# Second stage of a long convolution: one of the four spectral products goes to PSUM instead of SBUF

## Chip, cores and metric

The kernel runs on one core of one Trainium2 chip. The metric is the device time of one execution in microseconds, as the median of several executions.

## The reference, cut to what matters

```python
h_filt = (np.maximum(pos_emb @ w1, 0.0) @ w2) * np.exp(-0.01 * np.arange(S))[:, None]
u = x * v                                    # (2, 12480, 128)
Uf = np.fft.rfft(u, n=2 * S, axis=1)
Hf = np.fft.rfft(h_filt, n=2 * S, axis=0)
y = np.fft.irfft(Uf * Hf[None], n=2 * S, axis=1)[:, :S]
t = (x * y).reshape(B * S, D)                # 24960 tokens of 128
h = t @ w_in                                 # 128 -> 2048
out = (np.maximum(h, 0) + alpha * np.minimum(h, 0)) @ w_out
```

A long convolution per channel, done as a product of spectra, is followed by a two-layer network over all tokens. The change sits in the complex product `Uf * Hf`.

## The kernel before, in words

**Stages.** The transform has length 128 x 179 and is split by its two coprime factors, so that no twiddle step is needed between them. Stage 1 transforms over 179 and keeps frequencies `f` from 0 to 89 (`NF = 90`). Stage 2, for each `f`, transforms over 128, multiplies the spectra of data and filter, and stores the product again as two fp16 halves in the SBUF tile `z`. Stages 3 and 4 go back. The network of 32 token blocks and 16 slices of the hidden layer (lines 1247 to 1361) follows and takes most of the time. The 128 channels are worked on in two groups of 64, so there are two rounds of stage 2.

**Stage 2.** The function `stage2` (line 847) steps through the frequencies two at a time (`f0`). `skew` (line 151) writes out a software pipeline in program order. In each iteration it issues, in this order, `low`, `high`, `total`, `transform`, `neg`, `more` and `load`, each for a different `f0`: `low` for the pair that `transform` had three iterations before, `high` two before, `total` one before. One iteration holds:

- `transform`: 24 matmuls of 192 columns (lines 878 to 883) into a PSUM tile `p` of two banks. Bank 0 holds the real plane and bank 1 the imaginary plane, each with 256 columns of data (2 batches x 64 channels x 2 frequencies) and 128 of the filter. There are three such tiles, `mm`.
- `hidden` (line 894): ScalarE copies the filter part, scaled and repeated for both batches, to an SBUF tile `hs`.
- `product` (line 906): VectorE multiplies both planes of `p` by the real plane of `hs` into `ta`, then both planes by the imaginary plane of `hs` into `tb`. Each is one operation over 512 elements in each partition. `ta` and `tb` lie in SBUF (the tile named `ring` in the rows).
- `total`: `real` (line 911, GpSimd) subtracts `tb[1]` from `ta[0]`, and `imaginary` (line 916, VectorE) adds `tb[0]` to `ta[1]`; 256 elements each.
- `high` (line 929, ScalarE) and `low` (line 933, GpSimd) split the sum into two fp16 halves.
- `neg` (line 845, ScalarE) negates the table of sines for the transform two iterations on.
- `more`: one step of other work. In the first round it is `weights_in`, which rebuilds the network's first weights from their 64-bit words in `later(read, 6)` (four groups of six iterations; lines 592 to 598) and scales them in `later(halves, 3)` (four groups of three; lines 602 to 607). In the second round it is `unscale` (lines 1138 to 1153).

The first and last pairs need care. The last two pairs of a round are worked on in pieces by `end`, in an order that a small planner (`Plan`) fixed beforehand.

**PSUM.** Three tiles `mm` take two banks each, and `mb[0]` and `mb[1]` take one each. In stage 2 the first round writes columns 0 to 15 of `mb[0]` by matmul (line 598) and uses columns up to 47 on VectorE (line 618 and the helper `scales`). The second round writes columns 0 and 1 by matmul (line 1148) and copies them on VectorE (line 1153). `mb[1]` holds the words under repair.

**Order.** Every engine works through its own list in program order. No wait is written in the code: the framework places a wait where an instruction uses a tile that another engine has written or still reads.

Of the kernel before, what the change touches and what calls it, by code (L numbers as in the profile page):

```python
# [14 lines left out]
ALU = mybir.AluOpType  # L15
# [21 lines left out]
NU = B * CG  # L37
# [252 lines left out]
def body(ctx, tc, A, out, stop=None, dbg=None):  # L290
    nc = tc.nc
    sy, ac, ve, po, te = nc.sync, nc.scalar, nc.vector, nc.gpsimd, nc.tensor
# [34 lines left out]
    def units(u, n=1, p=128):  # L327
        assert u >= FIRST or u + n <= FIRST
        t, u = (ring, u - FIRST) if u >= FIRST else (first, u)
        return t[:p, u:u + n].rearrange("p u e -> p (u e)")  # L330
# [348 lines left out]
    def phase_a():  # L679
        ps = ctx_a.enter_context(tc.tile_pool(name="psa", bufs=1, space=PSUM))  # L680
        mm = [ps.tile([128, 1024], F32, name=f"mm{j}") for j in range(3)]
        mb = [ps.tile([128, 512], F32, name=f"mb{j}") for j in range(2)]
# [164 lines left out]
        def stage2(tu, au, bu, hu, nu, extra, loaded=0):  # L847

            st = {}
            tws = {}  # L850

            def load(f0):
                if f0 % FB == 0:
                    fb = f0 // FB
                    tws[fb] = table(tu, fb)
                    if fb >= loaded:
                        load_table(tu, fb)
# [6 lines left out]
            def transform(f0):  # L864
                ns = st.pop(("ns", f0))
                tw = tws[f0 // FB]
                x = f0 // 2
                p = mm[((NF - 2) // 2 - x) % 3].rearrange("p (a m) -> p a m", a=2)
                for j in range(2):
                    f1 = f0 + j  # L870
                    fi = f1 % FB
                    ch, cl, sh, sl = (tw[:, fi, m, :] for m in range(4))
                    nh, nl = ns[:, j, 0, :], ns[:, j, 1, :]
                    zc = [z[:, :, m, 0, f1, :] for m in range(2)]
                    zs = [z[:, :, m, 1, f1, :] for m in range(2)]
                    for pl, (ah, al, bh, bl) in enumerate(((ch, cl, nh, nl), (sh, sl, ch, cl))):
                        o = p[:, pl, :2 * NC].rearrange("p (b f c) -> p b f c", f=2, c=ZC)[:, :, j]
                        te.matmul(o, ah, zc[0], start=True, stop=False)
                        te.matmul(o, ah, zc[1], start=False, stop=False)
                        te.matmul(o, al, zc[0], start=False, stop=False)  # L880
                        te.matmul(o, bh, zs[0], start=False, stop=False)
                        te.matmul(o, bh, zs[1], start=False, stop=False)
                        te.matmul(o, bl, zs[0], start=False, stop=True)
                st["p", f0] = p, *(units(u[x % n]).rearrange("p (a m) -> p a m", a=2) for u, n in ((hu, 2), (au, 4), (bu, 2)))
                if f0 < NF - 4:
                    hidden(f0)
                    product(f0)

            def hidden(f0, b0=0, b1=NB):

                p, hs, _, _ = st["p", f0]
                h = p[:, :, 2 * NU:2 * NC]
                if b1 - b0 == NB:
                    ac.activation(hs.rearrange("p a (b m) -> p a b m", b=B), h.unsqueeze(2).to_broadcast([128, 2, B, 2 * CG]), AF.Copy, scale=2.0 ** -17)  # L894
                    return
                for b in range(B):
                    x, y = (min(max(k - b * NB // B, 0), NB // B) for k in (b0, b1))
                    if x < y:
                        at = b * 2 * CG
                        ac.activation(hs[:, :, at + x * 2 * ZC:at + y * 2 * ZC], h[:, :, x * 2 * ZC:y * 2 * ZC], AF.Copy, scale=2.0 ** -17)  # L900

            def product(f0, b0=0, b1=NB):
                p, hs, ta, tb = st["p", f0]
                m = slice(b0 * 2 * ZC, b1 * 2 * ZC)
                for t, a in ((ta, 0), (tb, 1)):
                    ve.tensor_tensor(out=t[:, :, m], in0=p[:, :, m], in1=hs[:, a:a + 1, m].to_broadcast([128, 2, (b1 - b0) * 2 * ZC]), op=ALU.mult)  # L906

            def real(f0, b0=0, b1=NB, e=po):
                _, _, ta, tb = st["p", f0]
                m = slice(b0 * 2 * ZC, b1 * 2 * ZC)  # L910
                e.tensor_tensor(out=ta[:, 0, m], in0=ta[:, 0, m], in1=tb[:, 1, m], op=ALU.subtract)  # L911

            def imaginary(f0, b0=0, b1=NB):
                _, _, ta, tb = st["p", f0]
                m = slice(b0 * 2 * ZC, b1 * 2 * ZC)
                ve.tensor_tensor(out=ta[:, 1, m], in0=ta[:, 1, m], in1=tb[:, 0, m], op=ALU.add)  # L916

            def total(f0):
                real(f0)
                imaginary(f0)  # L920

            def place(f0, b0, b1):

# [14 lines left out]
            def until(last, stage):  # L938
                return lambda f0: stage(f0) if f0 <= last else None

            skew(list(range(0, NF, 2)), (9, until(NF - 10, low)), (8, until(NF - 8, high)), (7, until(NF - 6, total)),
                 (6, until(NF - 4, transform)), (4, neg), (4, more), (0, load))

            def end(P):
# [3 lines left out]
                P.now, P.pace["end"] = ("end", 0), (-1e5, 0)  # L948
                room = {f0: P.buf("mm") for f0 in (NF - 2, NF - 4)}
                P.op("PE", 1990, lambda: transform(NF - 2), w=[room[NF - 2], "zh"])  # L950
                lows = []

# [3 lines left out]
                def some(what, f0, x=None):  # L956
                    b0, b1 = ((0, 1), (1, NB), (0, NB))[2 if x is None else x]
                    n, a, y = 4 * ZC * (b1 - b0), (f0, b0, b1), ("y", f0, x)
                    e, en = (ve, "DVE") if x == 0 or x and f0 == NF - 2 and what == "low" else (po, "POOL")
                    ns = dve_ns if e is ve else pool_ns  # L960
                    if what == "product":
                        op("ACT", act_ns(n, True) + 100 * (x == 1), lambda: hidden(*a), [room[f0]], [("hs", f0, x)])
                        op("DVE", 2 * dve_ns(n), lambda: product(*a), [room[f0], ("hs", f0, x)], [y, ("product", f0, x)])
                    elif what == "total":
                        op(en, ns(n / 2), lambda: real(*a, e), [y], [(y, 0)])
                        op("DVE", dve_ns(n / 2), lambda: imaginary(*a), [y], [(y, 1)])
                    elif what == "high":
                        op("ACT", act_ns(n), lambda: high(*a), [(y, 0), (y, 1)], [y])
                    else:
                        op(en, ns(n), lambda: low(*a, e), [y], [("low", f0, x)])  # L970
                        lows.append(("low", f0, x))
# [97 lines left out]
        with tc.tile_pool(name="pre", bufs=2) as pre:  # L1069
# [15 lines left out]
            if stop == 'p':  # L1085
                return
        end = stage2((7, 0, 3, 5), (18, 16, 17, 19), (20, 21), (22, 23), 14, weights_in(mb, 9, (11, 12, 13, 24), (2, 10), 2))
        for g in range(1, NG):
            P = Plan(mm=3, m=2, x=7, v=3, sq1=2, uhl=3, sn=2, gst=2)
            P.flow = 360 / 255  # L1090
            y = end(P)
            P.guard = {"sq1": [("product", f0, x) for f0 in (NF - 4, NF - 2) for x in range(2)]}
            later = stage1(P, g, True, dict(x=(13, 5, 6, 7, 8, 3, 4), v=(2, 0, 1), uhl=(10, 11, 12), sq1=(22, 23)))
            drain(paced(P, "h", islice(later, 3)))
            drain(paced(P, "s", stage3(P, g - 1, [lambda u=u: units(u, 4) for u in (14, 18)], lambda i: units((24, 9)[i]), y)), paced(P, "u", later))
            tables = (0, 3, 14, 16)
            P.op("DMA", 2 * dma_ns(128 * 4096), lambda: [load_table(tables, fb) for fb in range(2)], w=["tw"])
            P.after("x")
            P.after("v")
            negs = 22  # L1100
            raws = [ring[:, u - FIRST:v - FIRST + 1:v - u] for u, v in ((6, 7),)]
            for f0 in range(0, 2 * FB, 2):
                P.op("ACT", 520, lambda f0=f0: negate(tables, negs, f0), r=["tw"])
                P.after("sq1")
            P.pace.update(h=(-30228, 41505), s=(-14272, 7297), u=(23122, 6183))
            P.urge, P.patience, P.bias = 3.1, 0, 911
            P.run()
            rotate(P)
            if stop == 'r':
                return  # L1110
            end = stage2(tables, (8, 20, 21, 5), (9, 18), (10, 11), negs, chain([none] * 4, [lambda: load_words(raws, 0)], unscale(mb)), 2)
# [336 lines left out]
```

## Time and profile before

| what | value |
|---|---|
| median of 3 runs | 1636.32 us (1633.52 to 1636.78) |
| the profiled execution | 1634.51 us |
| its span, first to last instruction | 1632.7 us |
| mean granted TensorE clock | 0.982 of full speed |
| busy: TensorE, ScalarE, VectorE, GpSimd | 95%, 81%, 79%, 63% of the span |
| first round of stage 2 | about 143 to 243 us of the span |
| second round of stage 2 | about 374 to 461 us of the span |

The rows of the trace name an instruction by engine, line and tile. In the timeline's rows the first number is the start in microseconds from the span's start and the second the time taken, over all instructions of the row where `x2` or more stands at its end. A bracket gives how long the engine was idle before and what ended that. Instructions of one engine overlap a little, so the distance from start to start says more of the cost of a link in a chain than the duration does.

### The profile page before, as it was taken

What the parts mean: (1) busy time and instruction counts of PE and PEld (TensorE: products, weight loads), DVE (VectorE), ACT (ScalarE), POOL (GpSimd) and SP (SyncE); (2) the same over time, 40 slices, a digit from 0 to 9 for tenths busy, and PEclk for the clock granted to TensorE, in tenths of its full rate; (3) what the DMA queues carried; (4) which work ended last, traced back from release to release, by engine and by line L of the source; (5) the groups of instructions that cost most, each with busy time, mean ns of one, the idle gap of its engine ahead of it and who ended that gap; (6) DMA issues with size and microseconds to landing.
All of it is one profiled execution on the core that took longest, in us unless ns stands there. A gap on an engine that the chain in (4) does not pass through costs nothing.

```text
span 1632.7 us, 34281 instructions
## 1 busy us (share of the span) xinstructions
PE 1553.0 (95%) x13452; PEld 1094.6 (67%) x13452; DVE 1289.7 (79%) x1867; ACT 1328.3 (81%) x2203; POOL 1033.0 (63%) x728
## 2 busy tenths in 40 slices
PE   6888887999998999999999999999999999999998
PEld 3888887889987566666666666665666666666664
DVE  7898988998998777777777777777777777777775
ACT  5887786886876888888888888888888888888886
POOL 5697896987972665556655556555566555665554
PEclk8998998999999999999999999999999999999999
DMA  7353437775358321202112021220202202022000
GB/s 203 113 173 133 143 119 217 238 215 172 130 153 234 100 56 41 57 21 57 47 50 57 21 57 36 61 57 21 57 21 76 57 20 57 21 76 57 20 11 20
DMA packets 91663, 141.86 MB, mean 87 GB/s; under 512 B 7057, under 2 KB 59891, under 8 KB 90061
## 3 DMA queue, kind: packets, MB, share of 16 engines
q1 hardware_dynamic: 90525, 139.10, 29.6%
q8 instruction: 105, 1.72, 0.4%
q10 hardware_dynamic: 976, 0.57, 0.1%
q14 instruction: 57, 0.47, 0.1%
HBM read 99.02 MB, written 40.63 MB: 86 GB/s over the span
## 4 chain that ended last, share of the span: by engine, by line
PE 72%; DVE 13%; POOL 4%; issue 4%; ACT 3%; DMA 3%; SPq 0%; POOLq 0%; DVEq 0%; ACTq 0%
PE hp L1270 31%; PE o L1270 31%; DVE ring L906 5%; DVE ring L916 2%; DMA first<-in_xv 2%; POOL ring L758 1%; PE yp L280 1%; PE yp L281 1%; PE yp L282 1%; PE mm L1007 1%; PE mm L1009 1%; PE mm L1008 1%; POOL ring L749 1%; DVE ring L1024 1%; POOL ring L721 1%
## 5 line engine op out<-in xcount | busy, mean ns | idle before, releaser
L1347 POOL TENSOR_TENSOR g_lo<-ring,g_hi 128x780 f16<-128x780 f32 x288 | 480.9, 1674 | 474.0 <-ACT g_hi L1346 474.0
L1340 DVE SCALAR_TENSOR_TENSOR ring<-ring,keep,hp 128x780 f32<-128x780 f32 x512 | 524.8, 1025 | 268.1 <-ACT ring L1339 258.8
L1339 ACT ACTIVATE ring<-hp 128x780 f32<-128x780 f32 x512 | 418.7, 818 | 162.3 <-PE hp L1270 161.0
L1270 PEld LDWEIGHTS <-w 128*128 128x128 f16 x3840 | 368.5, 97 | 269.3 <-issue 13.4
L1270 PE MATMUL hp<-ah,w 128*128 128x390 f16 x1984 | 489.2, 328 | 0.3 <-DVE ring L1340 0.3
L1346 ACT ACTIVATE g_hi<-ring 128x780 f16<-128x780 f32 x512 | 433.5, 847 | 1.1 <-DVE ring L1340 1.1
L1270 PE MATMUL o<-g_hi,ring 128*128 128x390 f16 x1536 | 378.4, 328 | 1.1 <-ACT ot L1361 1.0
L1270 PEld LDWEIGHTS <-ring 128*128 128x128 f16 x2304 | 223.2, 97 | 160.4 <-issue 2.1
L1270 PE MATMUL hp<-alo,w 128*128 128x390 f16 x992 | 244.7, 328 | 0.8 <-DVE alo L363 0.8
L1347 DVE TENSOR_TENSOR g_lo<-ring,g_hi 128x780 f16<-128x780 f32 x224 | 230.2, 1028 | 0.0
L1270 PE MATMUL o<-g_lo,ring 128*128 128x390 f16 x768 | 189.6, 328 | 0.6 <-POOL g_lo L1347 0.6
L1250 POOL TENSOR_TENSOR gl<-gt,gh 90x1024 f16<-90x1024 f32 x62 | 153.5, 2475 | 1.3 <-ACT gh L1249 1.3
L906 DVE TENSOR_TENSOR ring<-mm,ring 128x512 f32<-128x512 f32 (+2 forms) x188 | 116.0, 656 | 16.4 <-ACT ring L894 16.3
L1270 PE MATMUL o<-g_hi,w 128*128 128x390 f16 x512 | 126.3, 328 | 0.0
L1007 PE MATMUL mm<-t,z 128*128 128x128 f16 x512 | 102.7, 233 | 10.2 <-ACT z L929 6.8
L933 POOL TENSOR_TENSOR z<-ring,z 128x512 f16<-128x512 f32 x88 | 105.6, 1201 | 3.4 <-ACT z L929 3.4
L1009 PE MATMUL mm<-t,z 128*128 128x128 f16 x512 | 101.8, 231 | 0.7 <-DVE z L933 0.7
L1008 PE MATMUL mm<-t,z 128*128 128x128 f16 x512 | 101.9, 231 | 0.0
L911 POOL TENSOR_TENSOR ring<-ring 128x256 f32<-128x256 f32 (+1 forms) x90 | 77.1, 857 | 31.2 <-DVE ring L906 30.9
L804 ACT ACTIVATE z<-mm 128x720 f16<-128x720 f32 (+1 forms) x99 | 73.6, 753 | 23.1 <-PE mm L794 22.0
L807 DVE TENSOR_TENSOR z<-mm,z 128x720 f16<-128x720 f32 (+1 forms) x99 | 85.2, 875 | 6.1 <-ACT z L804 5.8
L792 PE MATMUL mm<-t,ring 98*128 98x180 f16 x320 | 80.1, 254 | 10.1 <-DVE ring L520 3.1
(214 smaller groups left out, 3141.7 us busy)
## 6 DMA issues: line engine op xcount, KB each, us to landing
gt<-g_d SPq DMA_DIRECT2D x16, 1440.0 KB
g_d<-ring SPq DMA_DIRECT2D x28, 720.0 KB
ring<-in_tw SPq DMA_DIRECT2D x34, 512.0 KB
ring<-in_xv SPq DMA_DIRECT2D x72, 196.0 KB
xt<-in_xt SPq DMA_DIRECT2D x31, 390.0 KB
out_t<-ot SPq DMA_DIRECT2D x31, 390.0 KB
first<-in_xv SPq DMA_DIRECT2D x56, 196.0 KB
first<-in_tw SPq DMA_DIRECT2D x12, 512.0 KB
```

The costliest lines, as they stand in the source:

```text
L807: ve.tensor_tensor(out=zb[:, 1, :, x:y, cs], in0=pv()[:, :, x:y], in1=zb[:, 0, :, x:y, cs], op=ALU.subtract)
L906: ve.tensor_tensor(out=t[:, :, m], in0=p[:, :, m], in1=hs[:, a:a + 1, m].to_broadcast([128, 2, (b1 - b0) * 2 * ZC]), op=ALU.mult)
L933: e.tensor_tensor(out=zl, in0=v, in1=zh, op=ALU.subtract)
L1007: te.matmul(o, hi, t3[:, 0], start=True, stop=False)
L1008: te.matmul(o, hi, t3[:, 1], start=False, stop=False)
L1009: te.matmul(o, lo, t3[:, 0], start=False, stop=True)
L1250: po.tensor_tensor(out=dl, in0=src, in1=dh, op=ALU.subtract)
L1270: te.matmul(o[:, b, :TOK], w, d[:, b], start=start and n == 0, stop=stop and n == 2)
L1339: ac.activation(neg, h, AF.Relu, scale=-1.0)
L1340: ve.scalar_tensor_tensor(out=acts[n], in0=neg, scalar=keep[:, f:f + 1], in1=h, op0=ALU.mult, op1=ALU.add)
L1346: ac.activation(gh, a, AF.Copy)
L1347: (po if n % 2 or n % NFT == 0 else ve).tensor_tensor(out=gl, in0=a, in1=gh, op=ALU.subtract)
```

## The change

In the iterations before the last two pairs, `products` takes the place of `product`. The product `p[0] * hs[1]`, which only the imaginary sum reads, goes to columns 256 to 511 of the PSUM tile `mb[0]`, by an operation of its own. The other product with `hs[1]` becomes an operation of 256 elements too. The imaginary sum in `total` then adds `ta[1]` from SBUF and `cross` from PSUM.

```diff
             st = {}
             tws = {}
+            cross = mb[0][:, 2 * NU:4 * NU]
...
                 if f0 < NF - 4:
                     hidden(f0)
-                    product(f0)
+                    products(f0)
...
+            def products(f0):
+                p, hs, ta, tb = st["p", f0]
+                m = slice(0, 2 * NU)
+                ve.tensor_tensor(out=cross, in0=p[:, 0, m], in1=hs[:, 1, m], op=ALU.mult)
+                ve.tensor_tensor(out=ta, in0=p[:, :, m], in1=hs[:, :1, m].to_broadcast([128, 2, 2 * NU]), op=ALU.mult)
+                ve.tensor_tensor(out=tb[:, 1], in0=p[:, 1, m], in1=hs[:, 1, m], op=ALU.mult)
...
             def total(f0):
+                ta = st["p", f0][2]
                 real(f0)
-                imaginary(f0)
+                ve.tensor_tensor(out=ta[:, 1], in0=ta[:, 1], in1=cross, op=ALU.add)
```

`2 * NU` is 256. `product` and `imaginary` stay as they are for the last two pairs of a round. There are 43 pairs before them in each round, 86 in all.

## Rows read from the trace of the kernel before

**Rows 1.** The page, part 4: chain that ended last, by engine.

```profile
PE 72%; DVE 13%; POOL 4%; issue 4%; ACT 3%; DMA 3%; SPq 0%; POOLq 0%; DVEq 0%; ACTq 0%
```

**Rows 2.** Windows: stretch, its length, busy us (instructions) of each engine, PEclk, DMA share, GB/s.

```profile
143.00:205.00 62.00, 55.22 (x667) 53.39 (x666) 56.20 (x100) 47.45 (x89) 51.47 (x51) 1.00 0.40 137
205.00:243.00 38.00, 33.68 (x395) 32.38 (x393) 32.83 (x54) 32.58 (x69) 36.70 (x37) 1.00 0.36 118
386.00:461.00 75.00, 75.00 (x912) 75.00 (x910) 73.72 (x116) 61.23 (x114) 74.91 (x76) 1.00 0.36 116
```

**Rows 3.** Timeline of VectorE in round one, a group of six iterations.

```profile
174.30 1.29 DVE L906 TENSOR_TENSOR ring<-mm,ring 128x512 f32<-128x512 f32 x2 [1.75 <-ACT ring L894]
175.50 0.69 DVE L558 TENSOR_SCALAR mb<-mb 128x512 f32<-128x512 f32 x1
176.10 0.57 DVE L916 TENSOR_TENSOR ring<-ring 128x256 f32<-128x256 f32 x1
176.59 1.28 DVE L906 TENSOR_TENSOR ring<-mm,ring 128x512 f32<-128x512 f32 x2
...
182.37 0.67 DVE L567 SCALAR_TENSOR_TENSOR ring<-ring,mb 128x512 int32<-128x512 int32 x1
...
188.79 1.29 DVE L906 TENSOR_TENSOR ring<-mm,ring 128x512 f32<-128x512 f32 x2 [1.61 <-ACT ring L894]
```

**Rows 4.** Timeline of ScalarE, end of the same group.

```profile
187.01 0.65 ACT L592 ACTIVATE mb<-ring 128x512 f32<-128x512 f32 x1 [1.75 <-DMA ring<-in_wi]
```

**Rows 5.** Groups of VectorE by line and shape: busy us, mean ns, idle before.

```profile
L906 DVE TENSOR_TENSOR ring<-mm,ring 128x384 f32<-128x384 f32 x8 | 4.0, 546 | 0.0
...
L561 DVE TENSOR_SCALAR mb<-mb 128x512 int32<-128x512 int32 x4 | 2.7, 684 | 0.0
...
L906 DVE TENSOR_TENSOR ring<-mm,ring 128x128 f32<-128x128 f32 x8 | 1.9, 281 | 0.0
```

**Rows 6.** Timeline of VectorE in round two.

```profile
388.38 1.28 DVE L906 TENSOR_TENSOR ring<-mm,ring 128x512 f32<-128x512 f32 x2
...
460.07 1.27 DVE L906 TENSOR_TENSOR ring<-mm,ring 128x512 f32<-128x512 f32 x2
```

**Rows 7.** Timeline of TensorE in round two: the first of every six matmuls.

```profile
388.04 0.25 PE L878 MATMUL mm<-z,ring 128*128 128x192 f16 x1
...
440.02 0.25 PE L878 MATMUL mm<-z,first 128*128 128x192 f16 x1
```

**Rows 8.** Timelines of VectorE and TensorE early in the kernel.

```profile
23.30 0.30 DVE L455 TENSOR_SCALAR nb<-ones,n 128x128 f32<-128x128 bf16 x1
...
23.91 0.16 DVE L337 TENSOR_SCALAR sr<-mb 128x1 int32<-128x1 int32 x1
...
24.21 0.46 PE L468 MATMUL mb<-w2q,nb 128*128 128x128 f32 x2 [1.97 <-DVE sr L337]
```

**Rows 9.** Timelines of TensorE and ScalarE around the last group that reads words.

```profile
198.25 0.25 PE L598 MATMUL mb<-ones,first 128*128 128x1 bf16 x4 [1.11 <-ACT first L597]
...
204.99 0.58 ACT L894 ACTIVATE ring<-mm 128x512 f32<-128x512 f32 x1
```

**Rows 10.** Timelines of TensorE and VectorE at the start of round two.

```profile
384.53 0.60 PE L1148 MATMUL mb<-one,first 1*128 1x1 f32 x4 [0.91 <-DVE first L1144]
...
386.39 1.28 DVE L906 TENSOR_TENSOR ring<-mm,ring 128x512 f32<-128x512 f32 x2
```

**Rows 11.** Timeline of ScalarE: the filter's copy at the end of round one.

```profile
219.01 0.60 ACT L894 ACTIVATE ring<-mm 128x512 f32<-128x512 f32 x1 [0.17 <-PE mm L883]
...
233.62 0.58 ACT L894 ACTIVATE ring<-mm 128x512 f32<-128x512 f32 x1
...
241.07 0.58 ACT L894 ACTIVATE ring<-mm 128x512 f32<-128x512 f32 x1
```

**Rows 12.** Timeline of GpSimd at the end of round one.

```profile
238.47 1.34 POOL L933 TENSOR_TENSOR z<-ring,z 128x512 f16<-128x512 f32 x1
239.77 0.73 POOL L911 TENSOR_TENSOR ring<-ring 128x256 f32<-128x256 f32 x1
```

## The prediction, made before the change was run

> **What bounds the kernel now.** The chain that ended last comes first. TensorE holds 72% of it and VectorE 13% [rows 1]; nearly all of the TensorE share is the network, which this change does not touch. So only the two rounds of stage 2 can move, and the windows say how much is there. Round two is full: TensorE 75.0 us busy of 75, VectorE 73.7, GpSimd 74.9 [rows 2]. Round one has room: in its first 62 us TensorE is busy 55.2 and VectorE 56.2, in the next 38 us 33.7 and 32.8 [rows 2]. The timelines then tell which wait ends last.
>
> In round two the same matmul comes back from 388.04 to 440.02 after 105 sets of six, so 0.495 us a set and 1.980 us for the 24 matmuls of an iteration [rows 7]. VectorE's pair of products comes 36 times from 388.38 to 460.07, every 1.991 us [rows 6]. TensorE sets the pace; VectorE is slower by 0.011 us, 0.4 us behind at the end.
>
> The first 62 us of round one are groups of six iterations, 174.30 to 188.79, 14.49 us, where six transforms need 11.9 [rows 3, 7]. Four iterations carry a word operation of VectorE each, and the last, line 567, ends at 183.04 [rows 3]. Only then can the next words be loaded; ScalarE waits 1.75 us for them until 187.01 [rows 4], and what it has queued behind, the filter's copy for the next pair, starts the next group. So a group is 8.74 us of VectorE and 5.75 of load and ScalarE. After the words are read, groups of three iterations follow. Two of them take 219.01 to 233.62, 14.61 us [rows 11]; the copies of line 602 on ScalarE and the matmul of line 603, which waits for them, set these 7.3 us, and neither uses what the change moves.
>
> **VectorE's part of the change.** Two products of 512 start 1.20 us apart from the next instruction, so 0.60 each [rows 3]. The sizes 128 and 384 take 281 and 546 ns [rows 5], 1.035 ns an element, so 256 elements take 0.60 less 256 x 1.035 ns: 0.335 us from start to start. A new iteration has 0.335 + 0.60 + 0.335 = 1.27 for 1.20: **0.07 more**. Two prices are not in the trace. Writing the product to PSUM: 0.335 at the least, 0.60, a full product, at the most; I take 0.335, since line 561, which writes PSUM, takes 684 ns where line 906 steps and lasts about the same (1.29 for two overlapping) [rows 3, 5]. The sum from SBUF and PSUM: 0.335 at the least, as for a product of one operand from each, and 0.49 at the most, what the sum of line 916 steps now [rows 3]. Something holds up this sum of two SBUF operands while GpSimd works: in round two 1.991 - 1.20 = 0.79 us are left for it and its wait for an operand, far over 0.335 for its size, while the products, with one operand in PSUM, keep 1.27 to 1.29 a pair in both rounds [rows 3, 6]. I take 0.335. So the sum saves **0.155 us** in a word iteration and **0.45** in round two.
>
> **What this is worth where VectorE sets the pace.** From a group's start to the end of line 567 there are four products and three sums: 4 x 0.07 - 3 x 0.155 = -0.19 us. Three groups are followed by a load: **-0.6 us**.
>
> **A wait that the change adds.** Line 598's matmuls write columns of `mb[0]`, the bank that `cross` now shares. The trace shows how such a wait is placed [rows 8]: line 468 writes columns 0 to 127 of a tile `mb` from `nb`, ready at 23.60, yet it waits for line 337, which reads column 384 of that tile until 24.07, and starts at 24.21. So I take the order to be by bank: line 598, and line 1148 in round two, wait for the `cross` product that precedes them in program order, and 24 matmuls of the next transform stand behind them on TensorE.
>
> The Trainium skill bears on this ("PSUM — Partial Sum Buffer", section "PSUM bank collisions raise a hardware error"): two engines in one bank and 32-partition quadrant are to be kept apart by semaphores, whatever columns they use. By that rule the sum is the -0.2 us below; with waits by column it would be the first rival's -3.3.
>
> *Line 598, followed by a load (three times).* The sixth pair of a group now starts 10.43 us after the group's start (four iterations of 1.27 + 0.60 + 0.335 and one of 1.605); its `cross` ends about 0.4 later, at 10.85. TensorE then needs 0.15, one transform (1.98) and 0.25 to give ScalarE the next filter part at 13.2. ScalarE does not ask before it has the words and has split the pair before: in rows 3 and 4 that is about 0.65 us before the pair at 188.79 (the copy takes 0.58 [rows 9]), so near 188.1, 13.8 after the start, and 13.6 when the group is 0.19 shorter. So the load hides the wait with 0.4 us to spare: **0**.
>
> *The last group.* No load follows. Line 598 ran at 198.25 [rows 9]. With the group starting 0.6 earlier, at 188.2 for 188.79 [rows 3], `cross` ends at 199.0 and the matmul runs at 199.1, 0.8 late. The three transforms behind it end at 205.4, where ScalarE's copy began at 205.0 [rows 9]. So the next part begins **0.4 us late** (the 0.6 saved is in this figure).
>
> *Line 1148.* It ran at 384.53 behind line 1144; the pair of its iteration starts at 386.39 [rows 10] and `cross` ends near 386.8. TensorE stands 2.3 us longer, the next pair moves from 388.38 to about 390.2, **+1.8**.
>
> **The rest of round one.** The groups of three keep their pace. After 233.62 nothing of line 602 is left, and the next three copies of the filter, at best 1.98 us apart, take until 241.07 [rows 11]: 7.45 against 5.94. GpSimd is late there: lines 933 and 911 at 238.47 and 239.77 follow each other without a gap [rows 12]. Their 1.34 and 0.73 become about 1.16 and 0.60 without the sum of line 916, and the line 911 that ended at 240.50 ends near 239.2: **-1.3**. The last such sum ends the round **0.3** sooner.
>
> **The rest of round two.** 36 iterations at 1.980 instead of 1.991: **-0.4**. At the tail the last iteration is 1.27 + 0.335 long for 1.991: **-0.4**.
>
> **Sum:** round one +0.4 - 1.3 - 0.3 = -1.2; round two +1.8 - 0.4 - 0.4 = +1.0; together **-0.2 us**. Stage 3 and the second stage 1 start from these ends, so I pass it on in full. The profiled execution would take 1634.3 for 1634.51, and the median of the runs shown lies 1.8 above that: **1636.1 us**.
>
> **Rivals.**
>
> *Waits by column.* Then lines 598 and 1148 wait for nothing new. Round one: -0.6, the last group's four iterations -0.3, then -1.6 as above: -2.5. Round two -0.8. Sum -3.3: **1633.0**. Against it stands the wait of line 468 [rows 8].
>
> *The matmul wait is not hidden (slower).* It decides from the point where `cross` ends more than 0.4 us later than I put it, or where ScalarE is ready sooner. Then TensorE, not the load, sets the start of three groups. Line 598 comes 1.4 us later than now in its group (10.9 for 9.5 after the start); if that counts whole, three groups add 4.1 to the sum of -0.2: +3.9, **1640.2**. For it: six transforms fill 11.9 of 14.5 us and TensorE has no other slack. Against: 1.75 us of waiting for words [rows 4].
>
> *The prices at their upper end.* Product 0.60 and sum 0.49 make a word iteration 0.34 longer than now and round two 2.03 an iteration, over TensorE's 1.98: 16 x 0.34 + 36 x 0.05 + 1.0 = +8: **1644**. The two sizes measured speak against it [rows 5].
>
> *GpSimd gives back more.* Freed of line 916, the groups of three may also shorten, at most by what lies between 14.61 and two times 6.2 (three transforms and a matmul), 2.2 us a pair of groups; half of that twice gives -2.4: **1633.7**.
>
> **How the numbers follow.** Changes under 0.2% (3.3 us) can hardly be told from none here. Forecast 0.62; waits by column 0.10; wait not hidden 0.15; upper prices 0.03; GpSimd gives more 0.10. The likeliest is 1636.1, with 1634 to 1638.5 as its own range, two microseconds or so for the parts of its sum. The range that leaves out 2 in 10 reaches from the first rival, less 0.5 for the size of its parts, to the second: 1632.5 to 1640.2. The first rival lies on the bound of 3.3 us, so half of it counts as faster, and half of the last, whose parts may come out larger, with 0.02 from the forecast's edge: 0.12. The second and third rivals, less 0.02 for their near ends, are slower: 0.16. Same: 0.72.
>
> **What the profile will show.** Right: the sum of line 916's place near 0.42 us everywhere, the 256-element products near 0.41; line 911 near 0.6; line 598 and line 1148 waiting for VectorE's `mb` product; groups still near 14.4 us and ended by the load; round two's pairs 1.98 apart with VectorE idle for some 0.37 of them. Wrong: a `mb` product of 0.6 us; line 598 without a wait on VectorE; a group that starts when TensorE is done; a round two that starts no later.

## The result, and the profile after

The changed kernel takes 1644.15 us as the median of 7 runs (1641.72 to 1655.02); the kernel before, run beside it on the same chip, took 1633.8 (7 runs). The ratio is **1.0073, 95% interval 1.0054 to 1.0091**. The forecast was no change, with a range up to 1640.2 us, 0.24% over its base of 1636.32: the kernel is slower, and by more than the range allows.

The kernel before is called before here, the changed one after. The profiled execution of after took 1648.78 us, 4.6 over the median; its span is 1647.0 us. To see where the time came from, measure each round of stage 2 on ScalarE, from the start of its first filter copy (line 894 before, 895 after) to the start of its 43rd. What lies outside (the head before the first copy, the stretch between the rounds, the tail) differs by up to 6 us between profiles of kernels that are alike there, so only the two lengths are compared. In after the first round runs from 146.24 to 251.11 us, the second from 383.30 to 472.16:

| kernel | first round | second round | slow stretches | ratio to before, 95% interval |
|---|---|---|---|---|
| before | 98.53 | 85.61 | 0 + 0 | |
| after | 104.87 | 88.86 | 3 + 1 | 1.0073 [1.0054, 1.0091] |
| e1_own_bank | 99.03 | 84.75 | 0 + 0 | 1.0004 [0.9991, 1.0017] |
| e2_wait_only | 102.81 | 88.74 | 2 + 1 | 1.0046 [1.0029, 1.0063] |
| e3_filler | 100.59 | 87.26 | 0 + 0 | 1.0032 [1.0016, 1.0049] |
| e4_round2_free | 103.35 | 84.60 | 2 + 0 | 1.0034 [1.0018, 1.005] |
| e5_order | 101.93 | 90.39 | 2 + 1 | 1.0049 [1.0032, 1.0067] |
| e6_more_first | 107.18 | 88.90 | 3 + 1 | 1.0091 [1.0076, 1.0107] |
| e7_all | 105.87 | 84.60 | 2 + 0 | 1.0067 [1.0052, 1.0082] |
| e8_between | 95.37 | 86.93 | 0 + 1 | 0.9998 [0.9982, 1.0014] |
| e9_between_all | 92.95 | 83.93 | 0 + 0 | 0.9968 [0.9956, 0.9981] |
| e10_round2_only | 97.11 | 84.61 | 0 + 0 | 0.9997 [0.9986, 1.0009] |
| e11_between_before | 96.69 | 85.47 | 0 + 0 | 0.9992 [0.9983, 1.0001] |

The lengths are of one profile each. The column of slow stretches counts, for the first round + the second, how often TensorE ran at 1.2 GHz behind line 598 (of four times) and behind line 1157 (of one); both are explained below. Round one of one and the same program differs by about 1.5 us between profiles, for two reasons: its groups end with a load that takes longer or shorter (before 98.53, e10 97.11), and where line 598 waits, the clock falls behind some of the waits and not behind others (after 104.87 with three slow stretches, e4 103.35 with two).

After loses 6.34 us in the first round and 3.25 in the second. The windows over the same stretches as in [rows 2] show what became of the engines (columns: stretch, its length, then each engine's busy time and number of instructions, the granted TensorE clock, DMA share, GB/s):

```profile
143.00:205.00 62.00, 53.78 (x612) 52.71 (x611) 49.58 (x112) 44.27 (x81) 39.84 (x44) 0.94 0.35 123
...
386.00:461.00 75.00, 71.61 (x847) 71.22 (x845) 61.37 (x148) 57.12 (x105) 63.74 (x71) 0.98 0.36 127
```

VectorE and GpSimd are busy for less of both stretches than in [rows 2], and so is TensorE, whose clock averages 0.94 in the first 62 us. TensorE's waits between 140 and 480 us (who waits for whom: us in total, times, the longest) name the place:

```profile
PE mb L598 <- DVE mb L912: 10.1, 4, 2.6
...
PE mb L1157 <- DVE mb L912: 3.4, 1, 3.4
```

Both are the waits of [rows 9, 10]'s matmuls for the new `mb` product. Before the change, line 598 stood for ScalarE instead, and for 6.5 us less:

```profile
PE mb L598 <- ACT first L597: 3.6, 4, 1.1
```

TensorE's timeline of after shows what follows the new waits:

```profile
160.71 0.24 PE L598 MATMUL mb<-ones,first 128*128 128x1 bf16 x4 [2.62 <-DVE mb L912]
160.81 0.24 PE L879 MATMUL mm<-z,ring 128*128 128x192 f16 x1
160.89 0.24 PE L880 MATMUL mm<-z,ring 128*128 128x192 f16 x1
...
161.30 0.37 PE L884 MATMUL mm<-z,ring 128*128 128x192 f16 x1
161.46 0.37 PE L879 MATMUL mm<-z,ring 128*128 128x192 f16 x1
...
164.60 0.25 PE L881 MATMUL mm<-z,ring 128*128 128x192 f16 x1
164.69 0.25 PE L882 MATMUL mm<-z,ring 128*128 128x192 f16 x1
...
396.50 0.91 PE L1157 MATMUL mb<-one,first 1*128 1x1 f32 x4 [3.39 <-DVE mb L912]
...
397.63 0.37 PE L881 MATMUL mm<-z,ring 128*128 128x192 f16 x1
397.80 0.37 PE L882 MATMUL mm<-z,ring 128*128 128x192 f16 x1
```

The first matmuls behind the wait are 0.08 us apart, the next twenty 0.16, then 0.08 again. TensorE had stood 2.62 us, and the granted clock of 160.8 to 164.8 is 0.57 of full speed: most of this transform ran at 1.2 GHz instead of 2.4. ScalarE shows that this transform, and no longer the load, now starts the group:

```profile
161.62 0.63 ACT L592 ACTIVATE mb<-ring 128x512 f32<-128x512 f32 x1 [1.43 <-DMA ring<-in_wi]
...
164.65 0.60 ACT L895 ACTIVATE ring<-mm 128x512 f32<-128x512 f32 x1 [1.84 <-PE mm L884]
```

The words are there at 161.62; the filter copy waits for TensorE (line 884) until 164.65. The third group differs: behind its wait of 2.22 us the clock stays full (1.00 from 193 to 197 us), and the filter copy waits for TensorE for only 0.35 us. The three groups that a load follows last 16.38, 15.72 and 15.06 us, start to start of line 558, where before's lasted 14.47, 14.63 and 14.49; the one that no load follows 15.79 for 12.81.

VectorE (groups of instructions: busy us, mean ns of one, then the idle time before them; below it two starts of the timeline):

```profile
L913 DVE TENSOR_TENSOR ring<-mm,ring 128x512 f32<-128x512 f32 x86 | 58.5, 681 | 0.0
...
L912 DVE TENSOR_TENSOR mb<-mm,ring 128x256 f32<-128x256 f32 x86 | 37.2, 433 | 42.8 <-ACT ring L895 39.8
...
L914 DVE TENSOR_TENSOR ring<-mm,ring 128x256 f32<-128x256 f32 x86 | 35.7, 415 | 0.0
L929 DVE TENSOR_TENSOR ring<-ring,mb 128x256 f32<-128x256 f32 x86 | 35.4, 411 | 0.1
```

```profile
167.15 0.41 DVE L929 TENSOR_TENSOR ring<-ring,mb 128x256 f32<-128x256 f32 x1
167.66 0.43 DVE L912 TENSOR_TENSOR mb<-mm,ring 128x256 f32<-128x256 f32 x1
168.00 0.68 DVE L913 TENSOR_TENSOR ring<-mm,ring 128x512 f32<-128x512 f32 x1
```

The prices are as forecast: 433, 415 and 411 ns. But from the sum to the next `mb` product it is 0.51 us, where a 256-element operation otherwise lets the next one start after 0.34: VectorE waits for its own sum before it overwrites the columns that the sum reads. Word iterations are 2.38 us apart (2.29 before, 2.205 in the forecast).

### The profile page after: what moved, and what is told of

The parts are those of the page before. It is cut to its first block, busy times and chain, and to the rows that moved or that the text cites. A ratio compares the mean times of both kernels' runs of the same rounds, so it can differ in the third digit from the quotient of the medians.

```text
span 1647.0 us, 34371 instructions
## 1 busy us (share of the span) xinstructions
PE 1561.4 (95%) x13452; PEld 1102.7 (67%) x13452; DVE 1279.6 (78%) x1953; ACT 1330.0 (81%) x2203; POOL 1019.3 (62%) x728
## 4 chain that ended last, share of the span: by engine, by line
PE 76%; POOL 7%; DVE 7%; ACT 4%; DMA 3%; issue 2%; POOLq 0%; SPq 0%; ACTq 0%; DVEq 0%
PE hp L1279 31%; PE o L1279 30%; POOL z L942 3%; POOL ring L919 2%; PE mm L1016 1%; PE mm L1018 1%; PE yp L280 1%; PE yp L281 1%; PE yp L282 1%; PE mm L1017 1%; POOL ring L758 1%; DVE z L807 1%; POOL ring L749 1%; DMA first<-in_xv 1%; PE mm L794 1%
## 5 line engine op out<-in xcount | busy, mean ns | idle before, releaser
L942 POOL TENSOR_TENSOR z<-ring,z 128x512 f16<-128x512 f32 x88 | 101.7, 1156 | 4.1 <-ACT z L938 4.1
L919 POOL TENSOR_TENSOR ring<-ring 128x256 f32<-128x256 f32 (+1 forms) x90 | 65.1, 724 | 55.4 <-DVE ring L914 44.2
L792 PE MATMUL mm<-t,ring 98*128 98x180 f16 x320 | 80.7, 255 | 11.1 <-DVE ring L520 2.7
L794 PE MATMUL mm<-t,ring 98*128 98x180 f16 x320 | 80.5, 254 | 7.6 <-POOL ring L758 7.6
```

Of the source, the lines that this page charges most:

```text
L942: e.tensor_tensor(out=zl, in0=v, in1=zh, op=ALU.subtract)
```

## The experiments

**Theory 1:** line 598 and line 1157 wait by bank for the `mb` product, and the transform behind them, partly at 1.2 GHz, sets the start of the next pair. **The rival (theory 2):** VectorE's operations cost more than put, and that makes the rounds longer.

**The product in the pair's own tile.** `cross` goes to free columns of the pair's `mm` tile, 128 in each bank; `mb[0]` is as before.

```diff
-                ve.tensor_tensor(out=cross, in0=p[:, 0, m], in1=hs[:, 1, m], op=ALU.mult)
+                ve.tensor_tensor(out=p[:, :, 2 * NC:], in0=p[:, 0, m].rearrange("p (a m) -> p a m", a=2), in1=hs[:, 1, m].rearrange("p (a m) -> p a m", a=2), op=ALU.mult)
```

> The product goes to the 2 x 128 free columns of its own pair's PSUM tile instead of mb[0]; every VectorE operation of the changed kernel stays. Theory 1 (the bank shared with the matmuls of lines 598 and 1157 makes TensorE wait, and the transform behind the wait runs at half clock): both waits are gone, all of the loss with them, and the cheaper sum shows, 2 to 4 us under the kernel before, about 1630 to 1632. Theory 2 (VectorE's fourth operation and the writes to PSUM cost the time, iteration by iteration): nothing of that is removed, so it stays 6 us or more above the kernel before. The 0.18 us between sum and product should go under both, since the columns now rotate through three tiles.

The loss is gone: +0.5 us and -0.9 in the two rounds, and theory 2, which expected 6 us or more, is out. The expected gain of 2 to 4 us isn't there either, and VectorE's timeline shows a part of the reason:

```profile
163.83 0.41 DVE L929 TENSOR_TENSOR ring<-ring,mm 128x256 f32<-128x256 f32 x1
164.16 0.43 DVE L911 TENSOR_TENSOR mm<-mm,ring 128x256 f32<-128x256 f32 x1
164.69 0.69 DVE L912 TENSOR_TENSOR ring<-mm,ring 128x512 f32<-128x512 f32 x1
```

From sum to product it is 0.33 now, but 0.53 from that product to the next, which reads the banks just written. The 0.18 us has moved by one place, and word iterations stay at 2.40.

**The wait without the products.** The kernel before, with a copy of one column to `mb[0]` ahead of the unchanged products.

```diff
                     hidden(f0)
+                    ve.tensor_copy(mb[0][:, 511:512], st["p", f0][1][:, 0, :1])
                     product(f0)
```

> The kernel before, with products and sum as they were, and one copy of a single column from hs to column 511 of mb[0] ahead of each pair's products: it adds the shared bank and a VectorE operation of about 0.1 us, and nothing else. Theory 1: lines 598 and 1148 wait 2 to 3.5 us for the copy, the transform behind them runs at half clock, and the kernel is 7 to 11 us slower than before. Theory 2: 16 word iterations by 0.1 us and little else, 1 to 3 us slower.

```profile
PE mb L598 <- DVE mb L887: 8.6, 4, 2.5
...
PE mb L1149 <- DVE mb L887: 3.1, 1, 3.1
```

One column is enough: +4.28 us and +3.13, 7.4 of the 9.6 that after loses, with every product and sum as before. (Round one of e4, which has the products of after and as many slow stretches as this run, loses 4.82.) Theory 1 holds for the larger part.

**Work for TensorE during the wait.** The changed kernel with 40 more matmuls of 128 columns ahead of line 598 and 54 ahead of line 1157; nothing reads their results.

```diff
+                for _ in range(n):
+                    te.matmul(o, tws[f1 // FB][:, f1 % FB, 0, :], z[:, :4, 0, 0, f1, :], start=True, stop=True)
                 next(extra, lambda: None)()
```

> The changed kernel with 40 matmuls of 128 columns into free columns ahead of each of the four line 598 steps, and 54 ahead of line 1157, so that TensorE works during the wait; the wait's end stays where it is. Their results are not read. Theory 1 as stated, with the clock as the larger part: matmuls after the wait come 0.082 us apart instead of 0.16, 1.6 us back in each of four groups and 1.4 in round two, so 6 to 8 us under the changed kernel and 2 to 4 above the one before. A variant of it, that the wait alone costs and not the clock: no more than 1 us back. Theory 2: nothing back.

```profile
157.52 2.40 PE L949 MATMUL mm<-z,ring 128*128 128x128 f16 x40
160.30 0.24 PE L598 MATMUL mb<-ones,first 128*128 128x1 bf16 x4 [0.39 <-DVE mb L912]
```

The matmuls behind are 0.082 us apart. Line 598 runs no sooner in its group, yet the rounds lose only 2.06 and 1.65 us, 3.7 for 9.6: in this pair of profiles the slow clock after the waits was worth 5.9 us, the wait and VectorE the rest. The whole kernel stays 0.32% above before, some 5 us.

**The second round's turn elsewhere.** The changed kernel, with line 1157's columns in `mb[1]`, at 400 and 401, which nothing else uses in that round (VectorE's small operations of `unscale` use columns 0 to 383).

```diff
-                te.matmul(mb[0][:, b:b + 1], iv[:, b, :], one1, start=True, stop=True)
+                te.matmul(mb[1][:, 400 + b:401 + b], iv[:, b, :], one1, start=True, stop=True)
```

> The changed kernel with the second round's small matmul (line 1157) writing columns 400 and 401 of mb[1] instead of mb[0], so that round two shares no bank. Theory 1: round two loses its wait of 3.4 us and the slow transform behind it, 3 to 4 us back, some 6 us above the kernel before; round one is unchanged. Theory 2: no difference from the changed kernel.

Round two takes 84.60 us: 4.3 less than in after and 1.0 less than before. That one wait, with the slow transform behind it, was the whole loss of the round.

**The order of the products.** `ta`, `mb`, `tb`, so that 0.6 us lie between the sum and the product that overwrites its operand.

> The changed kernel with the three products in the order ta, mb, tb: 0.6 us of other work now stands between the sum that reads the mb columns and the next product that overwrites them. Theory 1 (the shared bank makes TensorE wait, and the transform behind the wait runs at half clock; VectorE's 0.18 us of waiting for its own sum only puts the wait later): word iterations 2.20 instead of 2.38 us apart, so the mb product ahead of line 598 starts 5 x 0.18 = 0.9 us sooner and 0.6 us later in its iteration, net 0.3 us; the wait of line 598 stays above 2 us and the 1.2 GHz stretch behind it stays. Round one 103.5 to 104.5 us from first to last filter copy (104.87 in the changed kernel, 98.53 in the one before), round two 88 to 89 (88.86): 1642 to 1644 us. Rival theory (VectorE's own wait is most of the loss): 20 word iterations give 0.18 us back each and round one is at or under 101 us, 1640 us or less.

```profile
147.34 0.41 DVE L929 TENSOR_TENSOR ring<-ring,mb 128x256 f32<-128x256 f32 x1
147.67 0.68 DVE L912 TENSOR_TENSOR ring<-mm,ring 128x512 f32<-128x512 f32 x1
148.27 0.42 DVE L913 TENSOR_TENSOR mb<-mm,ring 128x256 f32<-128x256 f32 x1
```

The sum now lets its successor start after 0.33, and word iterations are 2.19 apart. Round one lies between the two expectations, 2.9 us under after. But it has two slow stretches for after's three. Against e4, which has after's round one with two, it gains 1.4 us. That is about the most that theory 1 left to VectorE's wait for its own sum, less than the 3.6 us of the rival, and no more than the spread between profiles. Round two gets 1.5 us longer. Line 1157 waits 3.60 us instead of 3.39, which is 0.2 of it; behind the wait 33 matmuls run at 1.2 GHz instead of 17, which adds 1.3.

**The words' step ahead of sum and transform.** The changed kernel with `(4, more)` moved in the pipeline's list.

```diff
-(7, until(NF - 6, total)), (6, until(NF - 4, transform)), (4, neg), (4, more), (0, load))
+(4, more), (7, until(NF - 6, total)), (6, until(NF - 4, transform)), (4, neg), (0, load))
```

> The changed kernel with the step of the words moved ahead of the sum and the transform in each iteration (the same work, issued earlier by a transform and three products): lines 598 and 1157 then stand behind the mb product of the pair before, which ends an iteration sooner (2.38 us in round one). Theory 1: the wait of line 598 falls from 2.6 us to under 0.5, that of line 1157 from 3.4 to under 1.4, the transform behind them stays at 2.4 GHz (matmuls 0.082 us apart instead of 0.16); round one 99 to 101 us instead of 104.87, round two 85 to 86.5 instead of 88.86: 1635 to 1638 us. Word iterations stay at 2.38. Rival theory (VectorE's prices): nothing of VectorE's work changes, so 1643 to 1645 us.

The expectation rested on a mistake. The list is a cycle, as `skew` (line 105 of the kernel before) goes through it once per iteration: the edit moves all of the step by one pair, VectorE's part too, and line 598 is again behind the `mb` product of the transform it follows. It waits 10.1 us in 4, as in after. The groups of three become 7.83 us instead of 7.28. This run tells nothing between the theories.

**Both edits and the turn.** With the same mistake in it.

> Both of these edits together, and the turn of the scales written to columns of the other mb bank. If the two causes add up (bank wait with its slow clock, and VectorE's 0.18 us per iteration): word iterations 2.20 us apart, no wait over 0.5 us at line 598, groups of six back to the 14.5 us that the load of the inverse filter's words sets, the group that no load ends shorter than before's 12.81; round one 97.5 to 98.5 us (98.53 before), round two 84.6 to 85 (85.61 before): 1.0 to 2.0 us under the kernel before, about 1633 us. If the edits get in each other's way (the words' work issued earlier makes ScalarE or VectorE late instead), round one stays above 99 us and the time is that of before or more.

Round two is 84.60 us; round one has the waits (10.4 us in 4). But TensorE's timeline holds a comparison within one execution:

```profile
156.23 0.24 PE L598 MATMUL mb<-ones,first 128*128 128x1 bf16 x4 [2.60 <-DVE mb L913]
156.33 0.24 PE L879 MATMUL mm<-z,ring 128*128 128x192 f16 x1
156.41 0.24 PE L880 MATMUL mm<-z,ring 128*128 128x192 f16 x1
...
171.03 0.24 PE L598 MATMUL mb<-ones,first 128*128 128x1 bf16 x4 [2.66 <-DVE mb L913]
...
172.41 0.37 PE L882 MATMUL mm<-z,ring 128*128 128x192 f16 x1
172.57 0.37 PE L883 MATMUL mm<-z,ring 128*128 128x192 f16 x1
```

Behind 2.60 us of standing the clock stayed at 2.4 GHz (granted 1.00 from 155 to 165 us), behind 2.66 it fell (0.83 from 170 to 180). The first group lasts 14.79 us, the second 15.59. In both the filter copy that ends the group waits for TensorE (1.56 and 2.17 us), so it is the clock that makes the difference, not the load. The length of the stand doesn't decide the clock: behind 2.62 us in e4 and 2.47 in e2 it stayed full, behind 2.14 in e2 and 2.25 in e5 it fell. What decides is not shown by these runs.

**The words' step between transform and products.** Now TensorE's part keeps its place behind a transform, and VectorE's comes ahead of that pair's products.

```diff
+            def finish(f0):
                 if f0 < NF - 4:
                     hidden(f0)
                     products(f0)
...
+(6, until(NF - 4, transform)), (4, more), (7, until(NF - 6, total)), (6, until(NF - 4, finish)), (4, neg), (0, load))
```

> The changed kernel with the step of the words, and the sum, put between the transform of a pair and its filter copy and products (the transform's function is split in two for it). On TensorE lines 598 and 1157 still stand right behind the transform of a pair, but no longer behind that pair's mb product, only behind that of the pair before, which ends an iteration sooner. (The run before moved the step ahead of the sum and the transform: that moved VectorE's and TensorE's part of it alike, and the wait stayed at 2.6 us.) Theory 1 (TensorE waits by bank for the mb product, and the transform behind the wait may run at 1.2 GHz): the wait of line 598 for the mb product is under 0.5 us, matmuls behind it stay 0.082 us apart, the pair behind it comes about 4 us after the one before instead of 4.9 to 5.6, round one 99 to 101 us instead of 104.87, round two 84.8 to 86 instead of 88.86: 1635 to 1638 us. Rival (the prices of VectorE's operations): VectorE's order and operations are the same, so the time of the changed kernel, 1642 to 1645 us.

```profile
PE mb L598 <- DVE mb L914: 3.8, 4, 1.1
PE mb L1159 <- DVE mb L914: 1.4, 1, 1.4
```

The wait of line 598 falls from 10.1 to 3.8 us, about what before stood there for ScalarE, though the longest is 1.1 and not under the 0.5 expected; the granted clock of 143 to 205 us is 1.00. Round one takes 95.37 us, 9.5 less than after with the same operations on VectorE: the rival, which expected no change, is out for the larger part. Round one is shorter than before's too, which nothing had forecast. Round two takes 86.93 us, over the 84.8 to 86 expected: line 1159 (1157 in after) still waits 1.40 us, and behind this wait, too, the clock falls, to 0.69 from 382.3 to 386.3 us.

```profile
382.31 0.60 PE L1159 MATMUL mb<-one,first 1*128 1x1 f32 x4 [1.40 <-DVE mb L914]
...
384.46 0.37 PE L883 MATMUL mm<-z,ring 128*128 128x192 f16 x1
384.62 0.37 PE L884 MATMUL mm<-z,ring 128*128 128x192 f16 x1
```

**The same, with the order of the products and the turn.**

> The same with the products in the order ta, mb, tb (word iterations 2.19 us apart instead of 2.38, as the run with this order alone showed) and the turn of the scales in columns of the other mb bank. If bank wait, slow clock and VectorE's wait for its own sum are the whole loss, nothing of it is left: groups of six at 14.4 to 14.6 us, as before the change, ended by the load of the inverse filter's words; the group that no load ends at 12.3 to 12.6 instead of 12.81; round one 97.5 to 98.5 us (98.53 before), round two 84.5 to 84.9 (85.61 before): 1 to 2 us under the kernel before, which a ratio can hardly tell (1633 to 1635 us). If something else stands behind the loss, round one stays above 100 us.

```profile
164.24 0.41 DVE L931 TENSOR_TENSOR ring<-ring,mb 128x256 f32<-128x256 f32 x1
164.57 0.68 DVE L914 TENSOR_TENSOR ring<-mm,ring 128x512 f32<-128x512 f32 x1
165.17 0.42 DVE L915 TENSOR_TENSOR mb<-mm,ring 128x256 f32<-128x256 f32 x1
```

```profile
143.00:205.00 62.00, 57.19 (x697) 56.28 (x695) 54.65 (x130) 49.18 (x93) 48.31 (x53) 1.00 0.40 140
386.00:461.00 75.00, 71.26 (x862) 70.92 (x860) 63.84 (x155) 59.66 (x115) 69.59 (x75) 1.00 0.36 124
```

Word iterations are 2.19 us apart, the granted clock is 1.00 in both stretches, and the rounds take 92.95 and 83.93 us; the first is 2.4 under that of e8, from which it differs in this round by the order of the products alone. The kernel takes 1629.55 us as the median of 12 runs for 1634.63 (29 runs), ratio 0.9968 [0.9956, 0.9981]: **0.3% faster than before**, and so faster than after too. Both rounds are shorter than expected. Groups of six last 13.46, 14.18 and 13.20 us, less than the 14.4 to 14.6 that the load was taken to set. The product in PSUM is not the reason, since e11 (below) has them at 13.46, 14.25 and 13.42 without it. The order of the steps is the likelier one: for the words of the three loads ScalarE waits 2.2 us here and 0.8 in e11, for 5.4 in before.

**Only the second round.** The product of before in round one, the changed one in round two with its turn in `mb[1]`.

> The kernel before with the change in round two alone (round one keeps the product of 512 elements and the sum from the ring), and the turn of the scales in columns of the other mb bank, so that nothing else uses the product's bank then. Theory 1: round one as before, 98 to 99 us; round two 84.5 to 84.9 us instead of 85.61 (36 iterations at 1.980 instead of 1.991 and no wait at line 1157): 0.7 to 1.1 us under the kernel before in that round, about 1633 us, not to be told from no change in the ratio. Rival (the change costs on VectorE in any round): round two at or above 85.6 us.

Round two is 84.61 us, 1.0 less than before, as expected. Round one, with the same program as before, is 97.11 instead of the 98 to 99 expected: ScalarE waits 3.9 us for the words of the three loads, for 5.4 in before. The ratio can't show a gain of this size.

**The order of the steps without the change.** The products and sums of before in the order of e8.

> The kernel before (products of 512 elements in the ring, sum from the ring) with only the order of the steps of the run before: the step of the words and the sum between a pair's transform and its filter copy and products. It tells what the changed product itself is worth once nothing waits for it: that run took 92.95 us in round one and 83.93 in round two, this one has the same order without the product in PSUM. If the products carry the gain: round one 96 us or more, round two 85 or more, 1633 to 1635 us. If the order of the steps carries it (the read step's load is issued and its word product started sooner in the pair): round one 93 to 95 us with groups of six at 13.7 to 14.0, round two 84.5 to 85.5, about 1631 us; what is left to the product is then the difference, 3 x 0.1 us per group of six in round one and 36 x 0.011 in round two, some 2 us in all.

Both lengths are in the range of the first expectation: the products carry the larger part. Of e9's 7.3 us in the two rounds, 2.0 come with the order alone (98.53 to 96.69, 85.61 to 85.47) and 5.3 with the product in PSUM and the turn's place (96.69 to 92.95, 85.47 to 83.93). The 2.0 is little more than the spread between profiles, and e11's ratio can't be told from no change. The ratios, 0.9968 and 0.9992, are 0.24% apart, about 4 us. A part of that goes with GpSimd: in e11 its operations take 7.2 of the 7.44 us of a group of three, in e9 6.6 of 6.9.

## Why the prediction was wrong

**The prices of the operations: right.** 0.335 us from start to start for the new product, the shorter one and the sum; 36 pairs of round two 1.980 apart.

**The wait is placed by bank: right.** Lines 598 and 1157 wait for a product in other columns of their bank, 10.1 us in 4 and 3.4; one column did it in e2. So a wait by column is out. As `mb[0]` is one tile and one bank, these runs don't tell a wait by bank from a wait by tile. The rule of the Trainium skill that the prediction named ("PSUM — Partial Sum Buffer", section "PSUM bank collisions raise a hardware error") agrees with these rows.

**"So the load hides the wait with 0.4 us to spare: 0": this step failed.** It put line 598 at 10.85 us after the group's start and the next filter copy at 13.2. In after's first group, from 148.90 us, they come at 11.81 and 15.75. So the copy is 2.5 us late, and two terms make that up. *0.96 is VectorE's:* five iterations in which it waits 0.18 for its own sum, which no term of the sum had. *About 1.6 is the clock's:* 3.94 us from line 598 to the copy instead of 2.38 (0.15, one transform of 1.98 and 0.25), because the transform behind the wait ran mostly at 1.2 GHz, where the prediction had it at full speed without a reason. The load hides some of that: ScalarE stands 1.84 us for the copy, and the first group is 1.91 us longer than before's. The clock is the larger term: without its 1.6 us ScalarE would have stood some 0.3 us, and in the third group, where the clock stayed full, it stood 0.35 and the group is 0.57 us longer. The three groups together take +3.57 us for the -0.6 forecast. e3 isolates the clock. The order of the products, which takes VectorE's wait for its own sum away, is worth 1.4 us of round one in e5 against e4, and 2.4 in e9 against e8, where the spread between profiles is 1.5.

**The last group: 0.4 us late with the 0.6 saved, so +1.0 in its length. It was +2.98**, for the same two reasons: line 598 waits 2.63 us there, and the granted clock behind it is 0.64.

**Line 1148 (1157 after): +1.8, measured +3.5** (the pair behind it starts 5.50 us after the pair of its iteration, for 1.99). The added wait was nearly right: TensorE stands 3.39 us for 0.91, 2.5 longer where 2.3 was put. What was missing is again the clock: some sixteen matmuls at 0.16 us for 0.08 add 1.3.

**The end of round one: -1.3 and -0.3.** The last three filter copies take 6.68 us instead of 7.45: -0.8 for the -1.3; the -0.3 lies behind the last copy and was not measured. Line 933's place takes 1.16 us, as put, but line 911's 0.73, not 0.60. The groups of three kept 7.28 us, as put.

**The rivals.** "The matmul wait is not hidden" is what happened, at 0.15 when it deserved more: its own condition, `cross` more than 0.4 us late, was met by the 0.96 alone. Its price of +4.1 us left out the clock, so even it lay below the 9.6 that the two rounds lost. The other rivals are out: the waits are not by column, the prices are at their lower end, and GpSimd gave back no more than was put. (The last rival's 1633.7 is a slip: 2.4 less than 1636.1 counts the -0.2 twice, and 1633.9 would follow.) The medians are 10.4 us apart, and the ratio stands for near 12; what lies beyond the two rounds can't be placed with one profile.

## What to carry to other kernels

Free columns of a PSUM bank are not free if another engine uses that bank: list who else writes it in the same stretch, and give the product a bank whose users stand in the right order, or change that order, as e9 does. A stall of TensorE in a dense stretch can cost more than its length, because the transform behind it may run at half the clock; price it with and without, even for a stall of 1.4 us (e8). When an operation overwrites what its predecessor on the same engine reads, put another between them, and a loop's step can only be moved against its neighbours, not around the cycle.

## What the runs showed of the hardware

- **An engine waits for itself.** On VectorE an independent successor of a 256-element operation starts 0.33 us behind it, one that overwrites its operand 0.51 (after), one that reads the bank it wrote 0.53 (e1).
- **The length of a stall doesn't decide the clock.** 2.60 and 2.66 us of standing were followed by a full and a halved clock in one execution (e7). Stands of 1.40 (e8), 2.14 (e2) and 2.25 us (e5) were followed by a halved clock too, stands of 2.47 (e2) and 2.62 us (e4) by a full one.
- **An operand in PSUM takes the sum out of GpSimd's way.** The sum with both operands in SBUF took 0.57 us in the median of before's round one and 0.76 in round two; in after it takes 0.41 in both. The Trainium skill ("SBUF — State Buffer", section "Who interferes with whom") says that a VectorE instruction with two SBUF inputs contends with a GpSimd instruction that reads SBUF; the traces agree. GpSimd gains as well: line 911 took 0.91 us in the median over both rounds of before, its place in after 0.73. The 0.73 of [rows 12], from which 0.60 was worked out, stood already at that end.
